# Moving one line pair's folds by a step, and feeding the first weight column from a copy of its row

## The chip, the cores and the metric

The kernel runs on one core of one Trainium2 chip. The metric is the device time of one execution in microseconds (us), given as the median of several runs. The core has TensorE (PE in the profile), VectorE (DVE), ScalarE (ACT), GpSimd (POOL) and SyncE (SP); each works through its own list of instructions in order, and waits on semaphores where one engine needs another's result. SP, ACT and POOL also issue DMAs.

## The reference, cut to what matters

```python
batch, seq, dim, d_ff = 8, 3008, 256, 2048
X = np.fft.fft(x, axis=1)              # x: (8, 3008, 256)
x = np.fft.fft(X, axis=2).real         # (8, 3008, 256) -> (24064, 256)
h = x @ w_in                           # (24064, 2048)
g = h * np.cos(h)
out = g @ w_out                        # (24064, 256)
```

All of it is float32.

## The kernel before, in words

**Two parts.** The Fourier transform of a batch along its sequence is split in two halves, 64 by 47. The transform along `dim` is folded into `w_in` (the combined weights are `WC` and `WS`, made in the opening by `weights` and `keep_weights`). Symmetries halve the work: sums and differences of mirrored elements, called folds, are formed before the matmuls.

**The steps.** The main part is one list of 384 steps: 8 batches `b`, 6 column groups, 8 blocks of 256 hidden columns (`fp`). A step has two halves, `u` = 0 and 1. One turn `k` of the last loop of the kernel treats one half: it issues `mm1` (line 719, two matmuls `WC` and `WS`) for half k, rounding, sine and product on ACT and DVE for the halves just before, and `mm2` (line 810, seven matmuls for a step) for the half five turns back (`LAG`). Each step has eleven matmuls on PE. Before `mm2`, POOL forms four sums of a step's products in `sums` (lines 777, 783, 784, tile `S`); they are emitted in turn 2t + 3 for step t, and first read by PE in turn 2t + 5. Before `mm1`, ACT fills the accumulator by `seed` (line 700): it multiplies the row `nb` by one column of `wn`, the first row of `WS` turned upright. The first two halves use a matmul instead (`seed_first`, line 706, from the row copy `wrow`).

**The next batch's transform** runs between the steps of the present one. `transform(b)` makes a table: at step o (of the batch's 48) these calls are issued. Four line pairs p = 0 to 3 of the batch go through it. For each, `fold_x` (POOL, lines 377 and 384, tile `xf`) at two steps forms the sums that `pair_half` (PE, line 403, tile `pz`) multiplies some steps later; ACT copies the result to `zr` (line 414); `fold_z` (POOL, line 426, tile `zs`) folds that at two steps; `patch_z` sets two columns by two small ACT copies (`copy_small`, line 288); `store_pair` sends the result to DRAM (SP, line 489), for p = 0 with `store_ends`; `load_z` fetches it at steps 23 and 39. For the batches b = 2 to 7 the pair matmuls stand at steps 14, 17, 25 and 33 for p = 0 to 3, `fold_x` of p = 1 at steps 14 and 15, and `fold_z` of p = 0 at steps 14 and 15 too. For b = 1 all is shifted and these two do not meet. Calls of one step are issued in the order in which the table was filled; they stand at the step's end, behind `sums` and one piece of `combine_m` (POOL, lines 848 to 865, tile `cb`), which puts a finished column group together.

**The opening** (some 42 us) transforms batch 0, loads the weights and starts the steps. After the first 512 columns of `WS` are made, their first row is sent to `wn`, 128 elements to a column, by four DMAs from `WS` (line 991), two from POOL and two from SP. `clear_wn(0)` (POOL, line 646) then sets that row of `WS` to zero, which `mm1` needs before its first matmul with `WS`, and which must wait until the four DMAs have read it. Behind the clear POOL mixes weights (`mix_weights`, line 605). At step 0 of the table `opening` POOL runs `combine_w2` (four operations, line 685, tile `VX`: weights for `mm2`) and then `clear_wn(1)` for the next 512 columns. SP's list there is: the two `wn` DMAs, `load_w` for two quarters (line 240), `load_w2` twice (line 254), eight DMAs of `store_z` (line 468), more loads, `send_wn(2)` (line 643, the third quarter's row to DRAM), `load_z`, and `load_wn(2)` (line 649, back into `wn` columns 8 to 11).

Of the kernel before, what the change touches and what calls it, by code (L numbers as in the profile page):

```python
# [11 lines left out]
FP = mybir.dt.float32  # L12
# [119 lines left out]
def kernel(  # L132
# [7 lines left out]
    nc = tc.nc  # L140
# [11 lines left out]
    cpool = ctx.enter_context(tc.tile_pool(name="consts", bufs=1))  # L152
# [100 lines left out]
    def load_w2(f0, f1, eng=nc.sync):  # L253
        eng.dma_start(
            out=w2.rearrange("p (q c) -> p q c", c=ND)[:, 2 * f0 : 2 * f1],
            in_=moe_w_out.rearrange("(q p) c -> p q c", p=128)[:, 2 * f0 : 2 * f1],
        )
# [9 lines left out]
    WS = cpool.tile([128, NDFF], FP, tag="WS", name="WS")  # L267
    wn = cpool.tile([128, 16], FP, tag="wn", name="wn")
# [194 lines left out]
    def store_z(p, j0=0, j1=NJ, engs=(nc.sync, nc.sync)):  # L463
        half, q = divmod(p, 2)
        zd, zs = take_zd(0, half), zps[p][:, 0:1024]
        for e in range(2):
            p0 = 16 * e + XP * q
            engs[e].dma_start(
                out=zd[p0 : p0 + XP, 256 * j0 : 256 * j1].rearrange("i (y d) -> y i d", d=128),
                in_=zs[64 * e + 2 * j0 : 64 * e + 2 * j1, :].rearrange("y (i d) -> y i d", d=128),  # L470
            )
# [36 lines left out]
    def second_half(b, gs, pbs):  # L508
        for i, g in enumerate(gs):
            for q in range(4):  # L510
                jj = 4 * g + q
                at = 256 * i + 64 * ((q - 1) % 4 if g == 0 else q)
                for e in range(2):
                    rows = slice(64 * e, 64 * e + 64)
                    for h in range(2):
                        nc.tensor.matmul(  # L516
                            pbs[e][64 * h : 64 * h + 64, at : at + 64],
                            lhsT=z2s[b][rows, 128 * jj + 64 * h : 128 * jj + 64 * h + 64],
                            rhs=BJ[rows, 64 * jj : 64 * jj + 64],
                            start=i == 0 and q == 0,  # L520
                            stop=True,
                            skip_group_check=True,
                        )
        pq = spool.tile([128, 1024], FP, tag="pq", bufs=4, name="pq")
        nb = spool.tile([128, 512], FP, tag="nb", bufs=4, name="nb")
        for i, g in enumerate(gs):
            ready[b, g] = (pq[:, 512 * i : 512 * i + 512], nb[:, 256 * i : 256 * i + 256])
        return pq, nb
# [30 lines left out]
    def transform(b):  # L559
        todo = {}  # L560

        def at(o, *call):
            todo.setdefault(o, []).append(call)

        for p in range(4):
            sh = (5, 3, 3, 0)[p] if b == 1 else 5 if p == 0 else 0
            o = 8 * p + sh
            if p < 2:
                at(2 if b == 1 else p, turn_x, b, p)
            at(1 + p if b > 1 else max(2, 1 + p), load_xx, b, p)  # L570
            at(5 + p + (3 if b == 1 else 0), take_middle, b, p)
            for k in range(2):
                at(o + 6 + k, fold_x, b, p, k)
                at(o + 9 + k, fold_z, b, p, k)
            pairs[per * (b - 1) + o + 9] = b, p
            at(o + 11, patch_z, b, p)
            at(o + 12, store_pair, b, p)
            if p == 0:
                for e in range(2):
                    at(10 + e, fold_ends, e)  # L580
                at(o + 12, store_ends, b)
        at(23, load_z, b, 0)
        at(39, load_z, b, 1)
        for i in range(3):
            doubles[per * (b - 1) + (44, 46, 47)[i]] = b, (2 * i, 2 * i + 1)
        return todo
# [20 lines left out]
    def weights(e, n, tag="M", pw=None):  # L607
        pw = pw or psum("pw", tag)
        for o in range(2):
            at = 128 * e + 64 * o  # L610
            nc.tensor.matmul(  # L611
                pw[64 * o : 64 * o + 64],
                lhsT=CS[:, at : at + 64],
                rhs=mixed(n, o),
                start=True,
                stop=True,
            )
        return pw

    def keep_weights(e, n, pw, copy=nc.scalar.copy):  # L620
        W = WS if e else WC
        copy(out=W[:, 512 * n : 512 * n + 512], in_=pw)
# [13 lines left out]
    def keep_wn(n, pw):  # L636
        copy_v(out=wn[:, 4 * n : 4 * n + 4], in_=pw[:, 0:4])

    wds = {}

    def send_wn(n):
# [3 lines left out]
    def clear_wn(n):  # L645
        nc.gpsimd.memset(WS[0:1, 512 * n : 512 * n + 512], 0.0)  # L646
# [10 lines left out]
    ones = cpool.tile([1, 128], FP, tag="ones", name="ones")  # L657
    nc.vector.memset(VX[:, 0:512], 1.0)
    nc.vector.memset(ones, 1.0)
    wrow = cpool.tile([1, 256], FP, tag="wrow", name="wrow")  # L660
    scratch = cpool.tile([1, 128], FP, tag="scratch", name="scratch")
    nc.scalar.activation(out=scratch, in_=ones, func=AF.Sin, bias=0.0, scale=SIN_SCALE / 8)

    def keep_busy(pd, n, start):
        nc.tensor.matmul(  # L665
            pd[:, 0:n],
            lhsT=VX[:, 0:128],
            rhs=VX[:, 0:n],
            start=start,
            stop=True,  # L670
            skip_group_check=True,
        )
# [280 lines left out]
    copy_v = nc.vector.tensor_copy  # L953
# [27 lines left out]
    keep_busy(pds[0], 512, False)  # L981
    pw = [weights(1, 0)]
    keep_weights(1, 0, pw[0], copy_v)
    copy_v(out=wrow, in_=WS[0:1, 0:256])
    pw.append(weights(0, 0, "H"))
    keep_weights(0, 0, pw[1], copy_v)
    for n in (512, 512, 256):
        keep_busy(pds[0], n, False)
    for k in range(4):
        eng = nc.sync if k % 2 else nc.gpsimd  # L990
        eng.dma_start(out=wn[:, k : k + 1], in_=WS[0:1, 128 * k : 128 * k + 128])
    clear_wn(0)
    for q in (2, 3):
        load_w(q)
    load_w2(0, 2)
    load_w2(2, 4)
    for p in (1, 2, 0, 3):
        store_z(p, 4)
    load_w2(4, 6)
    load_bj(256, 512)  # L1000
    load_w2(6, 8)
    opening = {
        0: ((combine_w2, 0, 2), (clear_wn, 1)),
        2: ((load_bj, 512, NJ * 64), (combine_w2, 2, 4)),
        3: ((combine_w2, 4, 6, 0, 2),),
        4: ((combine_w2, 4, 6, 2, 4), (load_z, 0, 0, 8), (load_z, 0, 1, 8)),
# [27 lines left out]
    first = second_half(0, (0,), pbs)  # L1034
# [6 lines left out]
    for k in range(2 * n + LAG):  # L1041
# [5 lines left out]
        if cur:  # L1047
            if k % (2 * per) == 0:
                todo = transform(cur.s.b + 1) if cur.s.b + 1 < NB else {}
            if k >= AHEAD:  # L1050
                mm1(cur, 0)
                act_e(cur)
            if k == 0:
                for h in (cur, nxt):
                    mm1(h, 0)
                    seed_first(h)
                    act_e(h)
                spread_nb(0)
            if k < AHEAD - 1:
                mm1(cur, 1)  # L1060
# [129 lines left out]
```

## Time and profile before

| What | us |
|---|---|
| Median of three runs | 1919.11 (1918.76 to 1920.33) |
| The profiled execution's own time | 1918.31 |
| Its span, first to last instruction | 1916.4 |
| PE busy | 1903.2 (99% of the span) |
| POOL busy | 1441.7 (75%) |
| DVE busy, ACT busy | 1462.6, 1493.3 |
| PE waits for POOL, line 403 behind line 384 | 4.6, in six places |
| PE waits for POOL, line 719 behind line 646 | 1.1, in two places |
| Granted TensorE clock | 0.999 |

A profile is one execution. Matmuls overlap, and their ends are modelled, so that PE's busy share is not a share of its best rate; what matters is where PE starts late, and what it waited for. A line of the timeline has the start in us, the length in us, engine, line, operation, written tile and read tiles, shapes, the number of merged instructions, and in brackets the idle time of that engine before it with the instruction that ended it. In the chain of waits, the profile goes back from the last instruction, at each step to whatever released it.

### The profile page before, as it was taken

What the parts mean: (1) busy time and instruction counts of PE and PEld (TensorE: products, weight loads), DVE (VectorE), ACT (ScalarE), POOL (GpSimd) and SP (SyncE); (2) the same over time, 40 slices, a digit from 0 to 9 for tenths busy, and PEclk for the clock granted to TensorE, in tenths of its full rate; (3) what the DMA queues carried; (4) which work ended last, traced back from release to release, by engine and by line L of the source; (5) the groups of instructions that cost most, each with busy time, mean ns of one, the idle gap of its engine ahead of it and who ended that gap; (6) DMA issues with size and microseconds to landing.
All of it is one profiled execution on the core that took longest, in us unless ns stands there. A gap on an engine that the chain in (4) does not pass through costs nothing.

```text
span 1916.4 us, 32336 instructions
## 1 busy us (share of the span) xinstructions
PE 1903.2 (99%) x10412; PEld 1659.2 (87%) x10412; DVE 1462.6 (76%) x2536; ACT 1493.3 (78%) x3354; POOL 1441.7 (75%) x1784
## 2 busy tenths in 40 slices
PE   9999999999999999999999999999999999999998
PEld 5988889888988889888898888988889888898887
DVE  6777777778777777777777777777777777788787
ACT  4877778778787777778777787778777787788775
POOL 6888768887688776888768886688867888666775
PEclk9999999999999999999999999999999999999999
DMA  7612224122231223221241212502116021200001
GB/s 209 162 30 39 48 64 105 27 42 42 74 91 30 40 41 103 61 44 30 40 124 42 46 24 42 142 21 50 28 34 152 14 50 25 40 25 14 12 15 30
DMA packets 173222, 107.96 MB, mean 56 GB/s; under 512 B 112928, under 2 KB 152702, under 8 KB 171984
## 3 DMA queue, kind: packets, MB, share of 16 engines
q1 hardware_dynamic: 170488, 103.33, 23.9%
q8 instruction: 84, 1.38, 0.3%
q10 hardware_dynamic: 1848, 1.28, 0.3%
q0 software_dynamic: 720, 1.30, 0.2%
q14 instruction: 82, 0.67, 0.1%
HBM read 68.59 MB, written 48.39 MB: 61 GB/s over the span
## 4 chain that ended last, share of the span: by engine, by line
PE 94%; POOL 4%; issue 1%; DVE 0%; DMA 0%; ACT 0%; POOLq 0%; ACTq 0%; DVEq 0%
PE M L810 57%; PE H L719 33%; PE pz L403 2%; PE pb L516 2%; POOL zs L426 1%; POOL S L777 1%; POOL S L783 0%; POOL S L784 0%; PE pd L665 0%; PE pz L323 0%; POOL xf L377 0%; DMA wn<-WS 0%; PE M L451 0%; PE pw L611 0%; POOL cb L861 0%
## 5 line engine op out<-in xcount | busy, mean ns | idle before, releaser
L777 POOL TENSOR_TENSOR S<-r 128x512 f32<-128x512 f32 (+1 forms) x383 | 474.8, 1240 | 383.2 <-DVE r L761 329.3
L757 ACT ACTIVATE r<-r 128x512 f32<-128x512 f32 (+1 forms) x768 | 476.7, 621 | 249.6 <-DVE r L751 247.7
L751 DVE SCALAR_TENSOR_TENSOR r<-r,H 128x512 f32<-128x512 f32 (+1 forms) x768 | 518.9, 676 | 158.0 <-ACT r L747 132.7
L810 PE MATMUL M<-S,VX 128*128 128x256 f32 (+1 forms) x2304 | 625.5, 377 | 0.0
L761 DVE SCALAR_TENSOR_TENSOR r<-H,r 128x512 f32<-128x512 f32 (+1 forms) x768 | 519.0, 676 | 122.3 <-ACT r L757 79.9
L810 PEld LDWEIGHTS M<-S,VX 128*128 128x128 f32 x2304 | 434.0, 190 | 66.7 <-issue 18.2
L719 PE MATMUL H<-pq,WC 128*128 128x256 f32 (+1 forms) x1536 | 453.0, 377 | 0.0
L719 PE MATMUL H<-pq,WS 128*128 128x256 f32 (+1 forms) x1536 | 451.0, 375 | 1.1 <-POOL WS L646 1.1
L747 ACT ACTIVATE r<-H 128x512 f32<-128x512 f32 (+1 forms) x768 | 447.5, 583 | 0.9 <-DVE H L735 0.9
L735 DVE TENSOR_TENSOR H<-ew,H 128x256 f32<-128x256 f32 (+1 forms) x768 | 324.9, 423 | 151.1 <-PE H L719 93.9
L810 PE MATMUL M<-r,w 128*128 128x256 f32 (+1 forms) x1536 | 387.9, 375 | 0.0
L700 ACT ACTIVATE H<-nb,wn 128x256 f32<-128x256 f32 (+1 forms) x766 | 366.0, 478 | 1.5
L731 ACT ACTIVATE ew<-H 128x256 f32<-128x256 f32 (+1 forms) x768 | 287.2, 374 | 100.6 <-PE H L719 96.5
L810 PEld LDWEIGHTS M<-r,w 128*128 128x128 f32 x1536 | 300.6, 197 | 27.6 <-PE pw L611 0.8
L719 PEld LDWEIGHTS H<-pq,WC 128*128 128x128 f32 x1536 | 283.3, 190 | 44.9 <-ACT H L700 7.3
L719 PEld LDWEIGHTS H<-pq,WS 128*128 128x128 f32 x1536 | 290.6, 190 | 35.8 <-POOL WS L646 2.3
L783 POOL TENSOR_TENSOR S<-S,r 128x256 f32<-128x256 f32 (+1 forms) x383 | 275.4, 719 | 30.1
L784 POOL TENSOR_TENSOR S<-r,S 128x256 f32<-128x256 f32 (+1 forms) x383 | 274.8, 718 | 30.0
L810 PE MATMUL M<-r,VX 128*128 128x256 f32 (+1 forms) x768 | 225.4, 375 | 0.0
L810 PE MATMUL M<-S,w 128*128 128x256 f32 (+1 forms) x768 | 225.3, 375 | 0.0
L810 PEld LDWEIGHTS M<-S,w 128*128 128x128 f32 x768 | 150.5, 196 | 14.4
L810 PEld LDWEIGHTS M<-r,VX 128*128 128x128 f32 x768 | 146.0, 190 | 14.4
(94 smaller groups left out, 885.4 us busy)
## 6 DMA issues: line engine op xcount, KB each, us to landing
out_dram<-ob SPq DMA_DIRECT2D x724, 32.0 KB
xp<-in_x_dram SPq DMA_DIRECT2D x119, 128.0 KB
xp<-xr SPq DMA_DIRECT2D x112, 128.0 KB
z<-zd SPq DMA_DIRECT2D x56, 192.0 KB
xr<-in_x_dram SPq DMA_DIRECT2D x14, 752.0 KB
zd<-zs SPq DMA_DIRECT2D x98, 96.0 KB
nb<-nd SPq DMA_DIRECT2D x23, 256.0 KB
wr<-in_moe_w_in_dram SPq DMA_DIRECT2D x4, 512.0 KB
```

The source lines that it names most:

```text
L700: nc.scalar.activation(out=h.H[:, 0:T], in_=s.nb[:, 0:T], func=AF.Copy, bias=0.25, scale=wn[:, f : f + 1])
L719: nc.tensor.matmul(h.H[:, 0:T], lhsT=W[:, 128 * f : 128 * f + 128], rhs=s.pq[:, e * 256 : e * 256 + T], start=False, stop=True, skip_group ...
L731: nc.scalar.mul(out=h.ew[:, 0:T], in_=h.H[:, 0:T], mul=2.0)
L735: nc.vector.tensor_tensor(out=h.H[:, T : 2 * T][:, ::-1], in0=h.ew[:, 0:T], in1=h.H[:, 0:T], op=ALU.subtract)
L747: nc.scalar.activation(out=r, in_=y, func=AF.Copy, bias=BIG, scale=1.0)
L751: nc.vector.scalar_tensor_tensor(out=r, in0=r, scalar=-BIG, in1=y, op0=ALU.add, op1=ALU.subtract)
L757: nc.scalar.activation(out=r, in_=r, func=AF.Sin, bias=0.0, scale=SIN_SCALE)
L761: nc.vector.scalar_tensor_tensor(out=r, in0=y, scalar=-0.25, in1=r, op0=ALU.add, op1=ALU.mult)
L777: tt(out=sv[:, 0:2], in0=qv[:, 1:2].to_broadcast([128, 2, T]), in1=qv[:, 0:4:3], op=ALU.subtract,)
L783: tt(out=sv[:, 2], in0=sv[:, 1], in1=gv[:, 0, 0], op=ALU.subtract)
L784: tt(out=sv[:, 3], in0=gv[:, 1, 0], in1=sv[:, 2], op=ALU.add)
L810: nc.tensor.matmul(acc[key][m // 2][:, 256 * (m % 2) : 256 * (m % 2) + T], lhsT=w, rhs=a, start=first, stop=s.fp == 7, skip_group_check=True,)
```

## The change

Three things are done. In `transform`, the calls are entered in two passes: first, for all p, the `fold_x` calls (so that they come ahead of `fold_z` where both fall into one step), then the rest; and `fold_z`, `patch_z`, `store_pair` and `store_ends` of p = 0 come one step later. In the opening, `wrow` holds 512 elements of the row instead of 256, the four `wn` DMAs read from it instead of from `WS`, the DMAs for columns 0 and 1 are issued by SP behind the second `load_w2` and ahead of `store_z`, the one for column 2 by POOL and the one for column 3 by SP where the four stood. In the table `opening`, `clear_wn(1)` stands ahead of `combine_w2(0, 2)`.

```diff
+        def first(p):
+            return 8 * p + ((5, 3, 3, 0)[p] if b == 1 else 5 if p == 0 else 0)
+
         for p in range(4):
-            sh = (5, 3, 3, 0)[p] if b == 1 else 5 if p == 0 else 0
-            o = 8 * p + sh
             if p < 2:
                 at(2 if b == 1 else p, turn_x, b, p)
             at(1 + p if b > 1 else max(2, 1 + p), load_xx, b, p)
             at(5 + p + (3 if b == 1 else 0), take_middle, b, p)
             for k in range(2):
-                at(o + 6 + k, fold_x, b, p, k)
-                at(o + 9 + k, fold_z, b, p, k)
+                at(first(p) + 6 + k, fold_x, b, p, k)
+        for p in range(4):
+            o = first(p)
+            for k in range(2):
+                at(o + 9 + k + (p == 0), fold_z, b, p, k)
             pairs[per * (b - 1) + o + 9] = b, p
-            at(o + 11, patch_z, b, p)
-            at(o + 12, store_pair, b, p)
+            at(o + 11 + (p == 0), patch_z, b, p)
+            at(o + 12 + (p == 0), store_pair, b, p)
             if p == 0:
                 for e in range(2):
                     at(10 + e, fold_ends, e)
-                at(o + 12, store_ends, b)
+                at(o + 13, store_ends, b)
...
+    def move_wn(k, eng):
+        eng.dma_start(out=wn[:, k : k + 1], in_=wrow[:, 128 * k : 128 * k + 128])
...
-    wrow = cpool.tile([1, 256], FP, tag="wrow", name="wrow")
+    wrow = cpool.tile([1, 512], FP, tag="wrow", name="wrow")
...
-    copy_v(out=wrow, in_=WS[0:1, 0:256])
+    copy_v(out=wrow, in_=WS[0:1, 0:512])
...
-    for k in range(4):
-        eng = nc.sync if k % 2 else nc.gpsimd
-        eng.dma_start(out=wn[:, k : k + 1], in_=WS[0:1, 128 * k : 128 * k + 128])
+    move_wn(2, nc.gpsimd)
+    move_wn(3, nc.sync)
     clear_wn(0)
     for q in (2, 3):
         load_w(q)
     load_w2(0, 2)
     load_w2(2, 4)
+    for k in range(2):
+        move_wn(k, nc.sync)
     for p in (1, 2, 0, 3):
         store_z(p, 4)
...
-        0: ((combine_w2, 0, 2), (clear_wn, 1)),
+        0: ((clear_wn, 1), (combine_w2, 0, 2)),
```

## The prediction, made before the changed kernel ran

> **What bounds the kernel.** I read the chain of waits first, then PE's list of waits, then PE's and POOL's timelines around each wait.
>
> ```profile
> PE 94%; POOL 4%; issue 1%; DVE 0%; DMA 0%; ACT 0%; POOLq 0%; ACTq 0%; DVEq 0%
> ```
>
> The chain ends on PE for 94% of the span. In the steps nothing but PE counts: a step of eleven matmuls takes 4.75 us there. So time can come only from places where PE starts late, and PE's list of waits has them all:
>
> ```profile
> PE pz L403 <- POOL xf L384: 4.6, 6, 0.8
> PE pd L665 <- DVE VX L658: 1.5, 1, 1.5
> PE H L719 <- POOL WS L646: 1.1, 2, 0.6
> PE po L908 <- DVE cb L878: 0.3, 1, 0.3
> ```
>
> The columns are us in total, times, and the longest. Rows one and three are what the change touches: pair matmuls behind `fold_x`, and the first `WS` matmuls behind the clears. First row one. PE's timeline at the stalled pair (p = 1, batch 2), then the same place of p = 2, which has no stall:
>
> ```profile
> 347.95 0.60 PE L810 MATMUL M<-S,VX 128*128 128x256 f32 x2
> 349.31 1.09 PE L403 MATMUL pz<-xf,L 64*64 64x512 f32 x8 [0.77 <-POOL xf L384]
> 350.33 0.70 PE L810 MATMUL M<-S,VX 128*128 128x256 f32 x2
> ...
> 388.02 0.59 PE L810 MATMUL M<-S,VX 128*128 128x256 f32 x2
> 388.55 1.19 PE L403 MATMUL pz<-xf,L 64*64 64x512 f32 x8
> 389.67 0.70 PE L810 MATMUL M<-S,VX 128*128 128x256 f32 x2
> ```
>
> From one `mm2` pair's start to the next it is 350.33 - 347.95 = 2.38 us with the stall and 389.67 - 388.02 = 1.65 without: the stall costs 0.73, a little under the 0.77 of idle, since the matmuls behind it ran closer together. The six stalls repeat every 234.75 us, once in each of the batches 2 to 7. What POOL did before it:
>
> ```profile
> 339.64 0.67 POOL L861 TENSOR_TENSOR cb<-cb,mr 128x225 f32<-128x225 f32 x1
> 340.25 1.41 POOL L426 TENSOR_TENSOR zs<-zr 128x252 f32<-128x252 f32 x2
> 341.62 1.28 POOL L377 TENSOR_TENSOR xf<-xp 128x512 f32<-128x512 f32 x1
> 342.84 1.29 POOL L777 TENSOR_TENSOR S<-r 128x512 f32<-128x512 f32 x1
> ...
> 346.33 1.41 POOL L426 TENSOR_TENSOR zs<-zr 128x252 f32<-128x252 f32 x2
> 347.69 1.28 POOL L377 TENSOR_TENSOR xf<-xp 128x512 f32<-128x512 f32 x1
> 349.05 0.21 POOL L384 TENSOR_TENSOR xf<-xp 128x4 f32<-128x4 f32 x1
> 349.21 1.27 POOL L777 TENSOR_TENSOR S<-r 128x512 f32<-128x512 f32 x1
> ```
>
> Two steps each hold the sums, a combine piece, a `fold_z` (L426) and a `fold_x` (L377): some 6.1 us of POOL in a step of 4.75. POOL falls behind, and `fold_x` stands last.
>
> The opening, in the chain of waits between 20 and 45 us:
>
> ```profile
> 24.71 4.61 DMA wn<-WS
> ...
> 29.45 0.52 POOL WS L646
> 29.98 0.04 issue
> 30.02 0.65 PE H L719 x2
> ...
> 38.50 0.46 POOL WS L646
> 38.97 0.04 issue
> 39.01 1.06 PE H L719 x4
> ```
>
> The clear waits for the slowest `wn` DMA, PE for the clear: 0.64 idle at 30.02, and 0.45 at 39.01 behind the second clear, which follows `combine_w2`.
>
> **The folds, step by step.** The emitted order of the changed kernel has POOL at steps 14 to 16 as: sums, combine, `fold_x`; sums, combine, `fold_x` with L384, `fold_z`; sums, combine, `fold_z`. PE's list is unchanged. With the rows above: combine ends 340.25, `fold_x` ends about 341.6; step 14's sums 341.6 to 344.5 (2.9 for L777, L783, L784), combine to 345.15, `fold_x` to 346.4, L384 to 346.6. PE wants it at 348.55 (end of the pair of `mm2` begun at 347.95). The stall becomes 2 us of slack, and PE gets its 1.65 as with p = 2: 6 x 0.73 = **4.4 us**.
>
> What the moved `fold_z` (1.41 a step) now delays: its first half ends at 348.0, so step 15's sums start there instead of at 349.21; combine to 351.5, second half to 352.8. Step 16's sums started at 353.19 when DVE let them; DVE comes 0.73 earlier, 352.4, so they start at 352.8, 0.4 late. PE first reads them (in the second row of S matmuls after the pair, 358.64, less 0.73) at 357.9; the first sum is done at 354.1. Slack 3.8 us: no cost. By step 17 POOL waits for DVE again. `fold_x` at L377 has 1259 to 1292 ns over 56, L426 711 to 739 over 112, whatever stands beside them, so I let no price change with the move. If the slack were gone, each us beyond it would cost PE a us, seven times (b = 1 moves too, without a stall before).
>
> The two patch copies (0.18 and 0.19 us, overlapping: 0.2) go from the turn of pair p = 1, where ACT was crowded (351.51), to two turns on, where a sine (357.03) waited 0.32 for DVE and hides them. `store_pair` and `store_ends`, six SP issues (2.8 us at 360.68 to 363.43), come one step later; SP's next step with work is 20, `load_z` 23: no one waits. ACT's wait for `zr` (1.5 us, six times) goes with the stall.
>
> **The opening.** DVE's copy to `wrow` doubles: 0.28 before, and a 128x512 copy took 0.69, so 0 to 0.4 more, I take 0.25; behind it is the copy to `WC`, done at 23.63 and used at 26.72. POOL then issues one DMA (0.57) instead of two and clears (0.51) by 24.6. PE's first `WS` matmul then follows the matmul ending 29.38 at once: 0.64 gained. All PE does to 39 us follows without gaps, POOL's mixing ends at about 35.1 instead of 35.6 (its weights' loads are issued 0.6 earlier on SP), the clear by 35.6, so the second wait goes too. But the next late thing stands right behind: ACT's seed for the following `WC` matmul ran 38.94 to 39.38, that matmul began at 39.49. This seed hangs on PE through DVE and so comes 0.64 earlier, not 1.09. I count the second clear at 0 (its bounds: 0 to 0.45). `combine_w2` ends 0.5 behind the clear, 38.9, used at 42.1; the sums behind it are needed 2 us after their end.
>
> SP issues the transfer of column 0 that POOL had, at 0.58 to 0.59 each: its queue is 0.6 earlier to the second `load_w2`, then 0.6 later at `store_z`, `send_wn(2)` and `load_wn(2)`. That last was issued at 44.56 and the trace has its last piece landed at 46.66; the seed that reads it ran at 47.10, and PE used the seed at 48.07. With PE 0.64 earlier, the seed must end by 47.4; landing at 46.7 gives 47.2, in time; at 47.25 gives 47.7, a loss of 0.3. Near the stores SP was held (one issue took 2.58 us), so transfers pace it, not issues, and I take 0. The Trainium skill, "Trainium Kernel Development and Optimization", Key Constraints, says all queues share the same 16 DMA engines and several issuers save only issue time; by it the moved DMA costs 0.6 of issue at the very most, and the gain would be 0.3 instead of 0.64.
>
> The Trainium skill, "DMA: Bandwidth & Descriptors", Anatomy of one DMA, puts the fixed part of a DMA at about 2.0 us. By that the last of the four, issued by 25.3, would land at 27.3, the clear would end before PE came at 29.38, and the opening would give nothing (sum 4.4). The trace disagrees: POOL was held until 29.34, and I go by it. Opening: **0.64**, bounds 0.3 and 1.09.
>
> **Sum.** 4.4 + 0.64 = 5.0. The profiled execution took 1918.31 (span 1916.4 and 1.9 around it): 1913.3 after. The median of the runs stands 0.8 above it, 1919.11, so I predict **1914.1**. What this kernel's measurement can tell from no change is 0.2%, 3.8 us: faster means below 1915.3, slower above 1922.9.
>
> **Rivals.** (1) The opening gives nothing, because `wn` columns 8 to 11 or another DMA come later by as much: 1919.11 - 4.4 = 1914.7. For it: the 0.2 us between landing and need. Chance 0.08. (2) The pair of p = 1 meets a second wait just behind the first, say `pz`'s accumulators, still read by DVE's product, which ended at 348.54 where PE wanted 348.55. Then perhaps 0.4 of each 0.73 remains: 1919.11 - 0.64 - 6 x 0.33 = 1916.5. Against it: p = 2 and 3 have the same DVE order and no idle. Chance 0.06. (3) Slower: the sums become what PE waits for. `fold_z` now stands ahead of step 16's sums, and if POOL ran later there than the 3.8 us of slack, PE would stall at the S matmuls in each of 7 batches. To end over 3.8 us slower it needs (5.0 + 3.8)/7 = 1.3 us each, so sums 5.1 us later than worked out, more than three further folds. The narrow spread of the fold rows speaks against it. 1923 or more; chance 0.03. (4) The folds do not come apart as the text says: the emitted list shows that they do; 0.01, 1918.5.
>
> **How the numbers follow.** The forecast has 0.82. Its own range: both clears pay, 1919.11 - 5.5 = 1913.6, less the 0.35 by which the lowest run was under the median, 1913.2; opening at 0.3 gives 1914.4. To hold rival 1 with the 1.2 by which the highest run stood over the median: 1916.0. The range is 1913.2 to 1916.0. Faster: 0.82 and most of rival 1, less some noise, 0.86. Within 0.2%: rival 2, rival 4 and that noise, 0.11. Slower: 0.03.
>
> **What would show it.** Right: PE's list has no wait of L403 for a fold, the p = 1 place takes 1.65 us, batches repeat every 234.0 us, and the first `WS` matmul follows at about 29.4. Wrong: L403 waits for anything else, PE waits for an S tile, ACT's seed for the fifth step waits for a DMA, or the batch period is unchanged.

## The result, and the profile after

| | Kernel before | Changed kernel |
|---|---|---|
| Median of ten runs each, us | 1919.6 (1918.09 to 1921.9) | 1914.81 (1913.32 to 1915.55) |
| The profiled execution's own time, us | 1918.31 | 1913.32 |
| Its span, us | 1916.4 | 1911.5 |
| Granted TensorE clock | 0.999 | 0.999 |

The ratio of the changed kernel's time to the time before is 0.9974, with a 95% interval of 0.9964 to 0.9984. The forecast was 1914.1, in a range of 1913.2 to 1916.0.

The chain of waits in the profile of the changed kernel has lost its share of POOL and gained one of SP's DMA issues:

```profile
PE 98%; SPq 1%; DMA 0%; DVE 0%; issue 0%; ACT 0%; DVEq 0%
```

PE's list of waits (us in total, times, longest) no longer has the six waits of the pair matmuls for a fold, nor the two for the clears. A wait for ACT's seed is new in it. It is at the `WC` matmul behind the one that had waited for the second clear, where the prediction saw a seed as the next late thing:

```profile
PE pd L672 <- DVE VX L665: 1.5, 1, 1.5
PE po L915 <- DVE cb L885: 0.3, 1, 0.3
PE H L726 <- ACT H L707: 0.3, 1, 0.3
```

```profile
38.57 0.65 PE L726 MATMUL H<-pq,WC 128*128 128x225 f32 x2 [0.29 <-ACT H L707]
```

At the place of the old stall, PE's timeline of the changed kernel runs without a gap. From one `mm2` pair's start to the next it is 349.11 - 347.46 = 1.65 us, as forecast:

```profile
347.46 0.59 PE L817 MATMUL M<-S,VX 128*128 128x256 f32 x2
347.98 1.20 PE L403 MATMUL pz<-xf,L 64*64 64x512 f32 x8
349.11 0.70 PE L817 MATMUL M<-S,VX 128*128 128x256 f32 x2
```

POOL's timeline there shows why. `fold_x` (L377, L384) is done at 346.31, 1.7 us ahead of the pair matmuls. `fold_z` (L426) now stands behind it, in steps 15 and 16:

```profile
341.29 1.28 POOL L784 TENSOR_TENSOR S<-r 128x512 f32<-128x512 f32 x1 [0.25 <-DVE r L768]
...
344.75 1.28 POOL L377 TENSOR_TENSOR xf<-xp 128x512 f32<-128x512 f32 x1
346.10 0.21 POOL L384 TENSOR_TENSOR xf<-xp 128x4 f32<-128x4 f32 x1
346.26 1.40 POOL L426 TENSOR_TENSOR zs<-zr 128x252 f32<-128x252 f32 x2
347.62 1.28 POOL L784 TENSOR_TENSOR S<-r 128x512 f32<-128x512 f32 x1
...
351.09 1.41 POOL L426 TENSOR_TENSOR zs<-zr 128x252 f32<-128x252 f32 x2
352.45 1.29 POOL L784 TENSOR_TENSOR S<-r 128x512 f32<-128x512 f32 x1
```

In the opening, PE's first `WS` matmul starts at 29.17 instead of 30.02, without a wait; 0.14 of that is there already at the first `WC` matmul (26.58 instead of 26.72). But the chain of waits of the changed kernel, between 22 and 48 us, now goes through SP's issues and the third quarter's row on its way through DRAM, and ends in the seed of the fifth step:

```profile
27.02 0.97 SPq L644
...
28.03 1.35 SPq L644
...
40.29 4.46 DMA wd<-WS
44.78 0.03 issue
44.81 2.10 DMA wn<-wd
46.92 0.02 issue
46.94 0.46 ACT H L707
47.40 0.04 issue
47.44 0.65 PE H L726 x2
```

SP's two issues at L644 are the moved transfers of columns 0 and 1. They held SP for 2.36 us, from 27.02 to 29.38, where 1.2 had been counted. The two loads ahead of them (`load_w2`) took 1.09 us, though, where they had taken 2.28 before, so the stores behind started only 0.61 later than before (29.43 against 28.82), `send_wn(2)` 0.70 later (40.29 against 39.59) and `load_wn(2)` 0.25 later (44.81 against 44.56). ACT's timeline shows what hangs on the end of this chain: the seed waits 0.58 us for the transfer into columns 8 to 11. PE's matmul behind it is some 0.2 us late, too little for the list of waits.

```profile
46.94 0.45 ACT L707 ACTIVATE H<-nb,wn 128x225 f32<-128x225 f32 x1 [0.58 <-DMA wn<-wd]
```

### The profile page after: what moved, and what is told of

The parts are those of the page before. It is cut to its first block, busy times and chain, and to the rows that moved or that the text cites. A ratio compares the mean times of both kernels' runs of the same rounds, so it can differ in the third digit from the quotient of the medians.

```text
span 1911.5 us, 32335 instructions
## 1 busy us (share of the span) xinstructions
PE 1903.7 (100%) x10412; PEld 1658.2 (87%) x10412; DVE 1462.5 (77%) x2536; ACT 1494.6 (78%) x3354; POOL 1442.1 (75%) x1783
## 4 chain that ended last, share of the span: by engine, by line
PE 98%; SPq 1%; DMA 0%; DVE 0%; issue 0%; ACT 0%; DVEq 0%
PE M L817 60%; PE H L726 34%; PE pz L403 2%; PE pb L516 2%; PE pz L323 0%; SPq L468 0%; PE pd L672 0%; DMA wd<-WS 0%; PE M L451 0%; SPq L644 0%; SPq L254 0%; DMA zd<-zs 0%; DMA wn<-wd 0%; DVE cb L885 0%; SPq L240 0%
## 5 line engine op out<-in xcount | busy, mean ns | idle before, releaser
L817 PEld LDWEIGHTS M<-S,VX 128*128 128x128 f32 x2304 | 433.4, 190 | 67.2 <-issue 18.2
```

Source lines behind the costliest of these rows:

```text
L817: nc.tensor.matmul(acc[key][m // 2][:, 256 * (m % 2) : 256 * (m % 2) + T], lhsT=w, rhs=a, start=first, stop=s.fp == 7, skip_group_check=True,)
```

## The experiments

Two theories stood behind them. The first: the folds bring the whole measurable gain, some 4.3 us, and either the order or the later step would do. The second concerns the opening: what the earlier clears gain is lost again at the fifth step's seed, because the two moved DMAs hold SP. To measure the opening in a profile I use the stretch from the start of the first `WC` matmul to that of the tenth, the next one behind the `WC` matmul that needs the fifth step's seed: 23.26 us before (26.72 to 49.98), 22.87 in the changed kernel (26.58 to 49.45). It leaves out the time at which the first one starts, which differs by up to 1.2 us from profile to profile. All ratios are to the kernel before, with the 95% interval.

### The folds alone, and the opening alone

The first kernel has the new table with the old opening; the second the old table with the new opening. In short:

```diff
 # e1_folds_alone, against the changed kernel (wrow has 256 elements again)
...
-    move_wn(2, nc.gpsimd)
-    move_wn(3, nc.sync)
+    for k in range(4):
+        eng = nc.sync if k % 2 else nc.gpsimd
+        eng.dma_start(out=wn[:, k : k + 1], in_=WS[0:1, 128 * k : 128 * k + 128])
...
-    for k in range(2):
-        move_wn(k, nc.sync)
...
-        0: ((clear_wn, 1), (combine_w2, 0, 2)),
+        0: ((combine_w2, 0, 2), (clear_wn, 1)),
```

> The kernel before with the change of `transform` alone. My theory: the six stalls of the p = 1 pair go, 6 x 0.73 = 4.4 us, ratio 0.9977; PE's list of waits keeps the two waits of L719 for the clears (1.1 us), the batch period is 234.0 us. Rival (a second wait behind the fold): the pair keeps part of its 2.38 us, ratio 0.9985 or more. Rival (the opening is what paid): ratio 1.000.

> The changed kernel with the calls of `transform` as before, so that only the opening differs from the kernel before. My theory: the first WS matmul starts some 0.8 us earlier, 0.3 of which is lost again where ACT's seed waits for wn columns 8 to 11; PE ends 0.5 us earlier, ratio 0.9997, six stalls of 0.77 us remain. Rival (the opening saves all of 1.1 us of waits): PE at 60 us is 1.1 earlier, ratio 0.9994. Rival (it saves nothing): PE at 60 us where it was.

The folds alone came to 1914.55 us, a ratio of 0.9976 (0.9966 to 0.9986). The opening alone came to 1919.96, 0.9995 (0.9986 to 1.0004). PE's waits in the profile of the folds alone: none at L403, and a wait for a clear is back, one where two had been expected.

```profile
PE pd L669 <- DVE VX L662: 1.5, 1, 1.5
PE H L723 <- POOL WS L650: 1.1, 1, 1.1
```

It is the wait for the second clear, at 39.58. At the first `WS` matmul PE waited for nothing, although the opening is the old one: the first clear ended at 28.82, and the matmul followed 2.59 us behind the first `WC` matmul (27.34), as in the changed kernel, where it had been 3.30 before.

```profile
29.93 0.46 PE L723 MATMUL H<-pq,WS 128*128 128x225 f32 x1
```

PE's waits with the opening alone: the six are there, and the wait for the clear has turned into a wait for the seed.

```profile
PE pz L403 <- POOL xf L384: 4.5, 6, 0.8
PE H L722 <- ACT H L703: 1.6, 2, 1.3
```

So the folds carry the measured gain. The opening brought nothing that the times show; its stretch in this profile is 24.13 us, longer than before.

### The order alone, and the later step alone

Either edit to the folds was made without the other, with the new opening.

```diff
 # e3_order_alone, against the changed kernel
-                at(o + 9 + k + (p == 0), fold_z, b, p, k)
+                at(o + 9 + k, fold_z, b, p, k)
... (patch_z, store_pair and store_ends of p = 0 one step earlier, too)
```

```diff
 # e4_step_alone, against the changed kernel: one pass again
...
             for k in range(2):
-                at(first(p) + 6 + k, fold_x, b, p, k)
-        for p in range(4):
-            o = first(p)
-            for k in range(2):
+                at(o + 6 + k, fold_x, b, p, k)
                 at(o + 9 + k + (p == 0), fold_z, b, p, k)
```

> The changed kernel, but fold_z of p = 0 stays at steps 14 and 15 (with patch_z and store_pair as before); only fold_x is emitted ahead of it. Theory that POOL's order decides: step 14's sums start 1.2 us late behind fold_z, fold_x of step 15 ends with L384 at about 347.5 in the time of the changed kernel, PE wants it at 348.0: no wait of L403 or one of at most 0.2 us, ratio to before 0.9974 to 0.998. Theory that the later step is needed: L403 waits 0.5 us or more six times, ratio 0.999.

> The changed kernel, but the table is filled in the old order, so that in step 15 fold_z of p = 0 still stands ahead of fold_x; fold_z is at steps 15 and 16. Theory that POOL's load per step decides: step 14 holds one fold_x alone, step 15 fold_z 1.4 and fold_x 1.3 behind the sums, fold_x with L384 ends 1.4 later than in the changed kernel, at about 347.7, PE wants it at 348.0: no wait of L403, or up to 0.2 us; ratio 0.9974 to 0.998. Theory that the order is needed: L403 waits six times, ratio 0.999.

The order alone came to 1915.34 us (0.9974, 0.9963 to 0.9985), the step alone to 1915.43 (0.9973, 0.9962 to 0.9984). Neither profile has a wait of L403 for a fold. PE's and ACT's lists of the order alone:

```profile
PE H L726 <- ACT H L707: 2.9, 2, 2.6
PE pd L672 <- DVE VX L665: 1.5, 1, 1.5
```

```profile
ACT H L707 <- DMA wn<-wd: 3.1, 1, 3.1
```

Each of the two edits removes all six stalls by itself; the changed kernel has both, hence its slack of 1.7 us. What these two profiles also show is the seed's wait at its largest, 3.1 and 2.4 us, though nothing in the opening differs from the changed kernel. So its 0.58 there was one draw of a quantity that varies from profile to profile. PE lost 2.6 and 1.9 us by it in these two.

### Columns 0 and 1 elsewhere

Three kernels take the two DMAs away from their place behind the `load_w2` pair: behind `load_wn(2)`, on POOL behind the first clear, and in the old places (all four still from the copy of the row).

```diff
 # all three, against the changed kernel
-    for k in range(2):
-        move_wn(k, nc.sync)
 # e5_cols_later, in the last loop behind load_wn(2) and load_z
+            for j in range(2):
+                move_wn(j, nc.sync)
 # e6_cols_pool, behind clear_wn(0)
+    for k in range(2):
+        move_wn(k, nc.gpsimd)
 # e9_cols_in_place, where move_wn(2) and move_wn(3) stood
+    for k in range(4):
+        move_wn(k, nc.sync if k % 2 else nc.gpsimd)
```

> The changed kernel with the DMAs for wn columns 0 and 1 on SP behind load_wn(2) and its load_z instead of ahead of store_z. Profiles so far, from the first WC matmul to the tenth: before 23.3 us, folds alone 23.2, the changed opening 22.9, 24.1, 25.4, 24.9; ACT's seed waits 0.6 to 3.1 us for columns 8 to 11. Theory that the two DMAs ahead of the stores hold up SP's list: load_wn(2) is issued 18.0 us or less after the first WC matmul (18.2 to 20.6 with the changed opening), no wait of the seed, the stretch 22.6 us, ratio 0.997. Theory that the seed is late for another reason (wr or w2 loads earlier, transfers slow): the wait stays 0.6 us or more, the stretch 23.5 to 25.

> The changed kernel with the DMAs for wn columns 0 and 1 issued by POOL right behind clear_wn(0), so that SP has one wn DMA. If SP's list is what counts: as e5, stretch 22.6 us, no wait of the seed, ratio 0.997. If the 16 DMA engines' time counts, whoever issues: the seed waits as with the changed opening, stretch 23.5 to 25.

> The changed kernel with all four wn DMAs where they stood before (columns 0 and 2 from POOL, 1 and 3 from SP ahead of load_w), but reading from wrow, and the clears early as in the change. Theory: load_wn(2) is issued as early as before (17.8 to 18.4 us after the first WC matmul), the seed waits 0 to 0.4 us since PE comes 0.6 earlier, stretch 22.6 to 22.9 us, ratio 0.997. If clearing early itself is what delays: the seed waits 0.6 us or more.

They came to 1914.92 us (0.9971, 0.9961 to 0.998), 1915.02 (0.9972, 0.9961 to 0.9982) and 1914.24 (0.9972, 0.996 to 0.9983). The stretches are 22.93, 23.69 and 22.59 us, the seed's waits 0.6, 1.3 and 0.3. SP's timeline of the last, with the row's trip through DRAM behind it:

```profile
24.42 1.88 SPq L644 DMA_DIRECT2D wn<-wrow  x2
...
30.47 8.13 SPq L468 DMA_DIRECT2D zd<-zs  x8
...
40.74 0.31 SPq L650 DMA_DIRECT2D wd<-WS  x1
...
45.50 0.38 SPq L656 DMA_DIRECT2D wn<-wd  x1
```

The times do not tell these from the changed kernel. Two of the stretches are short, which is what the second theory asks for, but with the DMAs behind `load_wn(2)` the seed should not have waited at all, and with the DMAs on POOL the profile came out as the rival reading had it, in which it does not matter who issues them. One profile each, of a quantity that varies by 2.5 us under the changed opening alone, does not settle it.

### The slack behind the moved folds

The second `fold_z` of pair 0 is done six times instead of once, with the same result. This tests rival 3, and the slack of 3.8 us that the prediction had worked out ahead of PE's S matmuls.

```diff
 # e8_five_folds_more, against the changed kernel
             pairs[per * (b - 1) + o + 9] = b, p
+            for _ in range(5 if p == 0 else 0):
+                at(o + 11, fold_z, b, p, 1)
```

> The changed kernel with the second fold_z of p = 0 done six times in its step instead of once (same values), 7.0 us more of POOL in each of 7 batches. Theory (sums have 3.8 us of slack behind the moved fold): PE waits for S some 3.2 to 4 us in each of seven batches, the time is 23 to 28 us longer. If the slack were 0: 49 us longer. If POOL had 7 us to spare: no change.

One run: 1948.56 us. PE's list has the stall in all seven batches:

```profile
PE M L819 <- POOL S L786: 20.9, 7, 3.0
```

POOL's timeline has the six-fold `fold_z` of batch 2:

```profile
356.97 8.23 POOL L426 TENSOR_TENSOR zs<-zr 128x252 f32<-128x252 f32 x12
```

The twelve operations of L426 took 8.23 us instead of 1.41 for two, 6.8 more, and PE stalled 3.0: 3.8 us were slack, just as worked out. The price of a stall was not as worked out. The seven stalls are 20.9 us, but this execution is 35.2 longer than the profiled one of the changed kernel (1913.32). PE's timeline behind one stall, and the busy times in stretches of 4 us (in each row the stretch and its length, PE, PEld, DVE, ACT and POOL busy, the clock, and the DMA engines' share and GB/s):

```profile
366.48 1.02 PE L819 MATMUL M<-S,VX 128*128 128x256 f32 x2 [3.02 <-POOL S L786]
367.29 1.06 PE L728 MATMUL H<-pq,WC 128*128 128x256 f32 x2
```

```profile
364.00:368.00 4.00, 1.52 (x4) 1.26 (x5) 0.98 (x2) 0.61 (x1) 3.84 (x6) 0.84 0.42 104
368.00:372.00 4.00, 4.00 (x15) 3.35 (x15) 1.63 (x3) 2.38 (x6) 3.84 (x6) 0.73 0.04 11
372.00:376.00 4.00, 4.00 (x20) 3.55 (x19) 2.77 (x6) 3.10 (x9) 3.84 (x6) 1.00 0.02 4
```

A pair that takes 0.59 us elsewhere took 1.02 and 1.06: behind the stall PE ran at half clock. The two rows of 0.84 and 0.73 miss (0.16 + 0.27) x 4 = 1.72 us of full clock, so the half clock lasted 3.4 us. This happened behind six of the seven stalls, those of 2.93 to 3.04 us; behind the one in batch 1, of 2.84 us, the clock stayed at 1.0. The 35.2 us are made up so, by PE's start at the pair matmuls in this profile and in that of the changed kernel: 1.8 are there at the first pair of the main part, from the opening (98.06 against 96.22); batch 1 adds 4.0, with its stall of 2.8 and a wait at L403 of 0.9; and each of the other six batches adds 4.9, of which the stall of 3.0 and the half clock's 1.7 are 4.7. The rest, 0.2 in each of them, is unexplained. So a stall of 3.0 us cost 4.9.

### Again: the changed kernel, the folds alone, the columns in place

Because the opening varies from one execution to the next, these three were run once more, side by side.

> The changed kernel once more, beside the next three on one chip. Five profiles with its opening had the stretch from the first to the tenth WC matmul at 22.9, 24.1, 25.4, 24.9, 24.0 us, mean 24.3, against 23.3 and 23.2 with the opening before. Theory (the DMAs of columns 0 and 1 ahead of the stores cost more than the early clears bring): 24 to 25 us again, ACT's seed waits 1 us or more, the time equal to folds alone or up to 1 us longer. Rival (those profiles were odd draws, the opening saves 0.4 to 0.6): 22.6 to 22.9.

> The kernel before with the change of transform alone, again. Both theories: stretch 23.2 us. First theory: its time is equal to the changed kernel's or up to 1 us shorter. Rival: 0.5 us longer.

> All four wn DMAs where they stood, from wrow, clears early, folds as changed; one profile had 22.59 us. Theory: 22.6 to 22.9 again, seed waits under 0.5 us; the time 0.5 us under folds alone, 1 to 1.5 us under the changed kernel. If the first profile was a lucky draw: 23.5 or more.

They came to 1914.95 us (0.9974, 0.9963 to 0.9984), 1916.08 (0.998, 0.9971 to 0.9988) and 1914.62 (0.9975, 0.9966 to 0.9985). In the profiles the changed kernel's stretch is 25.40 us this time, with 2.6 of waiting in the seed; the folds alone have 24.34, the columns in place 23.45, with 1.2 of waiting in the seed. Two of the expectations missed: neither theory had the folds alone at more than 23.2, and the columns in place were to stay under 22.9. The times missed the first theory, too: the changed kernel is 1.1 us shorter than the folds alone, not equal or longer. The old opening varies as well. PE's list of the folds alone has its wait for the second clear at 2.3 us this time, and none for the first:

```profile
PE H L723 <- POOL WS L650: 2.3, 1, 2.3
```

All profiles by opening (the last row is the three kernels with the row copy whose SP list differs otherwise, the row-first one of the next section among them). The issues of `send_wn(2)` and `load_wn(2)` are counted from the first `WC` matmul:

| Opening | Profiles | Stretch, us | Mean | `send_wn(2)`, us | Mean | `load_wn(2)`, us | Mean |
|---|---|---|---|---|---|---|---|
| Old (before; folds alone, twice) | 3 | 23.26, 23.17, 24.34 | 23.6 | 12.87, 13.74, 13.37 | 13.3 | 17.84, 18.42, 17.41 | 17.9 |
| Changed (the changed kernel twice; opening, order and step alone; folds repeated) | 6 | 22.87, 25.40, 24.13, 25.43, 24.86, 24.03 | 24.5 | 13.71, 14.63, 14.08, 14.79, 15.28, 14.75 | 14.5 | 18.23, 20.57, 19.08, 20.56, 20.24, 18.95 | 19.6 |
| Row copy and early clears, DMAs in place (twice) | 2 | 22.59, 23.45 | 23.0 | 13.14, 13.82 | 13.5 | 17.90, 18.58 | 18.2 |
| Row copy and early clears, columns 0 and 1 later; on POOL; row first | 3 | 22.93, 23.69, 22.61 | 23.1 | 14.43, 13.54, 14.76 | 14.2 | 18.19, 18.73, 17.94 | 18.3 |

By the means, the copy of the row and the early clears bring about 0.6 us (third row against first), and the moved DMAs take about 1.4 (second against third). Both rest on few profiles whose values overlap, and so are not shown. In the eleven profiles with the early clears the stretch goes with the issue of `load_wn(2)`, from 22.59 us at 17.90 to 25.4 at 20.6; five of the six of the second row have it at 18.95 or later, and none of the other five. When `send_wn(2)` is issued does not decide it alone, since two kernels of the last row have it as late as the changed ones (14.43 and 14.76) and a short stretch all the same. The times lean another way: the medians of all runs of these kernels are 1915.5 for the folds alone (20 runs), 1914.9 for the changed kernel (18) and 1914.6 with the columns in place (16), each difference smaller than the spread of its runs. So what the new opening is worth as a whole stays open, even in sign, within about 1 us.

### The row ahead of the last weights

If SP's issues pace the seed, then taking the last `load_w2` out of SP's list ahead of `send_wn(2)` should bring the row sooner.

```diff
 # e10_row_first, against the kernel with the columns in place
     load_bj(256, 512)
-    load_w2(6, 8)
...
             load_wn(2)
+            load_w2(6, 8)
```

> As the kernel with all four wn DMAs in place, and the last load_w2 (512 KB, needed by POOL at about 55 us) behind load_wn(2) instead of ahead of send_wn(2). Theory (the row's round trip through DRAM is what comes last): load_wn(2) is issued 1 to 2 us earlier, 16 to 17 us after the first WC matmul, no wait of the seed, stretch 22.56, which is 23.2 less 0.64. If the wait for the row is not set by what stands ahead of it in the queue: load_wn(2) stays at 17.9.

It came to 1914.17 us (0.997, 0.9959 to 0.9982): the lowest median of all, and not to be told from the others. SP's timeline:

```profile
28.26 11.77 SPq L468 DMA_DIRECT2D zd<-zs  x8
...
42.25 0.24 SPq L650 DMA_DIRECT2D wd<-WS  x1
...
45.43 0.38 SPq L656 DMA_DIRECT2D wn<-wd  x1
```

With one issue fewer ahead of it, `send_wn(2)` came no earlier (14.76 us behind the first `WC` matmul): the eight stores ahead of it held SP for 11.77 us instead of 8.13 (9.45 in the second profile with the columns in place). The row then went through DRAM in 3.2 us instead of 4.8. The load was issued at 17.94, against 17.90 and 18.58 with the columns in place, where 1 to 2 less had been expected; the stretch was 22.61 us. So in this profile an issue taken out of SP's list was not its own length gained. That fits the view that transfers under way hold SP there, though one profile does not show it, and it speaks against the simple form of the second theory too, in which a moved DMA costs the time of its issue.

## Why the prediction was right, step by step

**The folds, 4.4 us.** Right in size, place and cause. From the first pair matmuls of the main part to the last transposes, PE gained 4.32 us in the profile: it stood 0.51 earlier at the first (96.73 became 96.22) and 4.83 at the last (1909.76 became 1904.93). That is six times 0.72, the batches repeat every 234.02 us, and the folds alone give the whole measured gain.

**POOL's times.** `fold_x` was worked out to end at 346.6 and ended at 346.31. Step 15's sums were to start at 348.0 and started at 347.62; step 16's at 352.8, and started at 352.45. All this is in the time of the kernel before, and PE was about 0.5 earlier here by the opening, so that `fold_x` came 0.2 to 0.3 later against PE than worked out, and its slack was 1.7 us instead of 2. The slack of 3.8 us ahead of the S matmuls is shown by the six-fold `fold_z`.

**What the moved step carries along.** ACT's six waits of up to 1.5 us ahead of the copy into `zr` are gone from its list, in which the longest there is 0.6 now, and the two patch copies (at 355.37) end ahead of the next sine (355.78). No one waits for the stores that SP issues a step later.

**The opening, 0.64 us.** Here the working failed in two places, though neither moved the time enough to push it out of the range. The first is the wait for the first clear, the 0.64 itself. In the profile of the changed kernel it is gone, as forecast. But of the three profiles with the old opening only the one that the prediction read has it. In the two of the folds alone the clear ended at 28.82 and 29.45, ahead of PE, which started its first `WS` matmul at 29.93 and 30.37 without a wait. The prediction had this case, in which the clear ends before PE comes, and dropped it because of one trace. The 2.0 us from which it worked the case out stand in the Trainium skill, "DMA: Bandwidth & Descriptors", Anatomy of one DMA, for DMAs that GpSimd issues, while the last of the four was one of SP's. What varied as well is the wait for the second clear, for which the prediction counted 0: it was 0.45, 1.12 and 2.28 us. With the changed opening neither clear is waited for in any profile, and PE waits 0.3 us for the seed that the prediction saw behind the second.

The second failed step is the sentence "transfers pace it, not issues, and I take 0", on what the moved DMAs do to columns 8 to 11. The sign that was named for this came true, a seed for the fifth step that waits for a DMA. It is in all six profiles with the changed opening, for 0.58 to 3.1 us, and in none with the old one. In the changed kernel's profile it cost PE 0.3 us: at the first `WS` matmul PE had gained 0.71 against the first `WC` matmul, and over the whole stretch 0.39. In others it cost PE 1.2 to 2.6 us. That the moved DMAs are the cause is argued and not shown: the seed also waits with these DMAs elsewhere (0.2 to 1.3 us in five profiles), since PE comes earlier there too. The Trainium skill, "Trainium Kernel Development and Optimization", Key Constraints, says that all queues share the DMA engines and that several issuers save only issue time. By that rule the prediction put the cost of the move at 0.6 us of issue at most. In the profile of the changed kernel the two issues measured 2.36 us, but what stood behind them came 0.61 us later at the stores, 0.70 at `send_wn(2)` and 0.25 at `load_wn(2)`, near that bound. In the five other profiles of this opening `load_wn(2)` came 1.1 to 2.7 us later than before, counted from the first `WC` matmul, more than that bound; how much of it is the move's own is not shown.

**The sum.** In the two first profiles the terms came out as 4.32 and 0.51 of a gain of 4.99 us in the profiled executions' own times, near the 5.0 forecast. That 0.51 was luck: 0.14 of it is the earlier start of the first `WC` matmul, and the stretch behind that ranges over 2.5 us from one profile of this opening to the next. The median of 1914.81 lies 0.7 above the forecast and 0.1 from rival 1, in which the opening gives nothing. Most of that is the starting point, though: the forecast went from 1919.11, the median of three runs, and that of ten is 1919.6. The gain by the medians of ten is 4.8, between the 5.0 forecast and rival 1's 4.4, and the runs cannot tell the two apart. The opening alone, which changed nothing that the times show (ratio 0.9995), speaks for rival 1, so that 0.08 was too low a chance for it.

**The other rivals.** Rival 2, a second wait behind the fold, is refuted by 1.65 us and by PE's list. Rival 3 needs sums that come later than the slack; they did not, but its price per stall was too small where stalls are long: 3.0 us of stall cost 4.9, by the half clock shown above. Rival 4 falls with POOL's timeline.

## What to carry to other kernels

A stall that recurs once a batch, with a neighbour place that lacks it, gives its price without any model: take the difference of the two places, and look which two calls meet there in one step of an engine with too much to do. A wait in the opening that one profile shows can be missing from the next. This opening, with its many queued DMAs, varied by 2.5 us, more than its edits are worth; take several profiles of either side, and of the kernel before ahead of pricing such a wait. Count a DMA moved onto a busy queue by when the issues behind it start, not by its own length: here the moved pair took 2.36 us, and the stores behind it began 0.61 later. Where a later need stands 0.2 us behind a landing, give the case in which it is missed a real chance.

## What the runs showed of the hardware

**A stall of 3 us costs more than itself.** Behind six stalls of 2.93 to 3.04 us PE ran at half clock for 3.4 us, about 1.7 us more for each; a stall of 2.84 us in the same run, and those of 0.77 us in the kernel before (granted clock 0.999), did not lower the clock. The Trainium skill, "TensorE: Matmul & The Clock Gate", Part 1, tells of a half rate after an idle window of about 3.4 us, and of free-running windows. The half rate and the 3.4 us agree with this trace; the idle stretch that set it off was a little shorter here, 3.0 us.

**Issuing a DMA can take long.** On SP, one `store_z` issue took 3.13 us (30.59 in the chain of waits of the changed kernel), and the two DMAs of 0.5 KB each took 2.36 together behind the loads, against 0.57 for the one that SP issued ahead of them. In six profiles of this opening the two took 2.05 to 2.95 us.
